# Weights requested by ScalarE, gradient rows requested two blocks ahead, and the inverse transform's last stage moved into the final tiles of the last chunk

## The chip, the cores and the metric

One core of one Trainium2 chip. The metric is the device time of one execution in microseconds. The engines are named as the profile names them: PE (TensorE, matmul), DVE (VectorE), ACT (ScalarE), POOL (GpSimd) and SP (SyncE, which here only requests transfers).

## The reference

The kernel computes a forward pass and its gradient. For x of 2048 tokens and D = 576 columns:

```python
xn = _layernorm(x)
out = x + S4(xn) + FFN(xn)
# S4: K = Re sum_n C exp(dt A l) dt B;  y = irfft(rfft(xn) * rfft(K)) + xn * Dskip
# FFN: h = relu(xn @ W_gate) * (xn @ W_up);  h @ W_down   (F = 4608)
out, vjp = jax.vjp(f, x, A_re, A_im, B_re, B_im, C_re, C_im, log_dt, Dskip, W_gate, W_up, W_down)
return out, *vjp(grad_out)
```

So there are 13 outputs: out (out_0), the gradient of x (out_1), those of the S4 parameters, and those of the three weight matrices.

## The kernel before

The work is written as two Python generators, and the main function takes from them in turns. `Ffn.gen` gives the feed-forward part, `S4.gen` the convolution; each `yield` hands over an estimate of the time of what was just written. After each piece of the FFN the main function takes pieces of S4 while S4's estimated time is behind `PACE` times the FFN's. The scheduler of the framework then orders each engine's instructions by itself, by the order of the program, the tiles' dependencies and the buffers of the pools; every transfer that an engine requests stands in that engine's order, and a request that has to wait holds up what stands behind it.

The FFN runs over 12 chunks of Fc = 384 hidden columns (three blocks ft of 128) and in each over 4 groups of 512 tokens. `load_w` (L211) requests a chunk's weights (five transfers), one chunk ahead, into one of two buffers. `a_unit` (matmuls at L254) makes the gate, the up projection and the gradient of h; `t_unit` (L278) transposes its results; `outdx` (matmuls at L296, 18 of 288 columns per tile of 128 tokens) adds a token tile's part of out and dx to `acc_dram` by a GpSimd transfer that accumulates. The weight gradients of a chunk follow at the start of the next one: `dw_down` four times (q = 0 to 3; 48 matmuls of 144 columns each, L316), `dw_gu` four times (L330, 32 matmuls of 384 columns) and `dw_left` (L346, which ends the chunk's work; its last one ends the kernel's matmuls). Each of these nine blocks requests its own rows, `gq_dram[q]` (L307) or `xs_dram[k]` (L326, L342), into a tile `rows` of the pool `ffn_d`, which has three buffers.

S4 is a convolution by discrete Fourier transforms of 16 x 256 points, done as matmuls in stages, with blocks that go out to DRAM and come back transposed between the stages (A, S, C). Everything is done for two halves of the columns, hf = 0 and 1, of DH = 288. `p1(hf)` transforms xn and the output gradient and ends with the gradient of the kernel K, `dk_dram`; `p2(hf)` makes K and the gradients by the parameters (`turn`, L880/L890; `sums`, L903 to L908, one turn per SC = 32 columns); `p3(hf)` multiplies in the frequency domain and transforms back. A last stage is a matmul pair of S3 and a block of C (`back2`, L658). `both` (L971) deals two of these out side by side by estimates of their lengths: p2(0) with p1(1) by W1, p2(1) with p3(0) by W3. p3(1) and `grads` come last. In p3's last stage (L733 to L751), for each half and each of 16 tiles, `base` = x + xn * Dskip + y (and the like for the gradient) is made on DVE from the pair in PSUM and stored to `base_dram` in FP32.

In the last chunk S4 is drained at the first outdx (the mark "last"), and from the third outdx on `final_tile(t)` is called, two tiles behind. It loads `f_base` (L1007), `f_acc` (L1009) and `f_xg` (L1011), adds, stores out (L1015), applies the layernorm's gradient, and stores dx (L1026). Tiles 10 to 15 are called between the last four dw_down and dw_gu.

`Balance.copy` decides by sums of estimates whether a copy out of PSUM goes to DVE (L62) or ACT (L68). PSUM has pools of 4 (`ps_mm`), 2 (`ps_s`, that of S4) and 2 (`pt`) banks.

Of the kernel before, what the change touches and what calls it, by code (L numbers as in the profile page):

```python
# [14 lines left out]
P = 128  # L15
# [7 lines left out]
ST = 16  # L23
# [11 lines left out]
PACE = 0.95  # L35
W1, W2, W3 = 56.0, 400.0, 91.0
# [145 lines left out]
class Ffn:  # L182
    def __init__(self, g, ctx, Wg, Wu, Wd, dWg, dWu, dWd):
# [20 lines left out]
        self.X = {}  # L204
        tail = D - (NK - 1) * P
# [5 lines left out]
    def load_w(self, c):  # L211
        nc = self.g.nc
        f0 = c * Fc
        nfull = NK - 1
        tail = D - nfull * P
        for w, W in ((self.wgs[c % 2], self.Wg), (self.wus[c % 2], self.Wu)):
            nc.sync.dma_start(w[:, 0:nfull, :], W[0:nfull * P, f0:f0 + Fc].rearrange("(k p) f -> p k f", p=P))
            nc.sync.dma_start(w[:tail, nfull, :], W[nfull * P:D, f0:f0 + Fc])
        nc.sync.dma_start(self.wds[c % 2][:, :, 0:D], self.Wd[f0:f0 + Fc, :].rearrange("(t p) d -> p t d", p=P))
# [102 lines left out]
    def dw_gu(self, c, k):  # L322
        g, nc = self.g, self.g.nc
        f0 = c * Fc
        xs = self.dp.tile([P, ST, 144], BF16, name="rows")
        nc.sync.dma_start(xs[:, :, 0:P], g.xs_dram[k][:])  # L326
# [8 lines left out]
    def dw_left(self, c):  # L335
# [5 lines left out]
        xs = self.dp.tile([P, ST, 144], BF16, name="rows")  # L341
        nc.sync.dma_start(xs[:, :, 0:W], g.xs_dram[k][:])  # L342
# [116 lines left out]
class S4:  # L459
    def __init__(self, g, aps, outs, Dskip):  # L460
# [8 lines left out]
        self.dk_dram = two("dk_dram", [P, ST, DH])  # L469
# [3 lines left out]
        self.base_dram = d("base_dram", [P, ST, 2, D], F32)  # L473
# [189 lines left out]
    def p1(self, hf):  # L663
# [28 lines left out]
        with ExitStack() as c:  # L692
            bp = self.pool(c, f"p1_c{hf}", 3)
            for n2 in range(ST):
                S3 = self.dft(bp, self.s3_dram, n2)
                Ct = bp.tile([P, 1, 2, DH], BF16, name="bC1")
                nc.sync.dma_start(Ct[:], self.C[1][hf][:, n2])
                o = bp.tile([P, DH], BF16, name="dk_o")
                g.bal.copy(o[:], self.back2(S3, Ct, 0), DH)
                nc.sync.dma_start(self.dk_dram[hf][:, n2, :], o[:])  # L700
                yield 0.3

    def p3(self, hf):
# [26 lines left out]
        with ExitStack() as c:  # L732
            cp = self.pool(c, f"p3_c{hf}", 1)  # L733
            dsk = cp.tile([P, DH], BF16, name="dsk")
            nc.sync.dma_start(dsk[:], self.Dskip[cols].rearrange("(o d) -> o d", o=1).to_broadcast([P, DH]))
            bp = self.pool(c, f"p3_d{hf}", 2)
            for n2 in range(ST):
                S3 = self.dft(bp, self.s3_dram, n2)
                Ct = bp.tile([P, 2, 2, DH], BF16, name="bC2")
                nc.sync.dma_start(Ct[:], self.C[2][hf][:, n2])  # L740
                xt = bp.tile([P, 3, DH], BF16, name="xt")
                nc.sync.dma_start(xt[:, 0, :], g.x_v[:, n2, cols])
                nc.sync.dma_start(xt[:, 1:3, :], g.xg_dram[:, n2, :, cols])
                o = bp.tile([P, 2, DH], F32, name="base")
                v.tensor_tensor(o[:], xt[:, 1:3, :], dsk[:].unsqueeze(1).to_broadcast([P, 2, DH]), op=ALU.mult)
                v.tensor_tensor(o[:, 0, :], o[:, 0, :], xt[:, 0, :], op=ALU.add)
                for i in range(2):
                    v.tensor_tensor(o[:, i, :], o[:, i, :], self.back2(S3, Ct, i), op=ALU.add)
                nc.sync.dma_start(self.base_dram[:, n2, :, cols], o[:])
                bal.add(d=1.8)  # L750
                yield 1.8  # L751
# [408 lines left out]
```

## Time and profile before

| what | value |
|---|---|
| median of 9 runs | 2060.55 us (2054.33 to 2063.26) |
| profiled execution | 2058.33 us |
| its span | 2056.6 us |
| mean granted clock | 0.972 |
| DMA, mean | 181 GB/s, 372.86 MB |

The profile is one execution, and its times count from the start of the span. A group's line gives the line, engine, operation and tile names, then the count, the busy time in us and the mean in ns, and behind the second bar the idle time of that engine just before these instructions and what ended most of it. In a line of windows, the numbers behind the times are busy us of PE, PE's weight loads, DVE, ACT and POOL. The chunks end, by dw_left, at about 199, 413, 595, 753, 908, 1069, 1226, 1388, 1542, 1726, 1897 and 2050 us, counted at the start of that work.

### The profile page before, as it was taken

What the parts mean: (1) busy time and instruction counts of PE and PEld (TensorE: products, weight loads), DVE (VectorE), ACT (ScalarE), POOL (GpSimd) and SP (SyncE); (2) the same over time, 40 slices, a digit from 0 to 9 for tenths busy, and PEclk for the clock granted to TensorE, in tenths of its full rate; (3) what the DMA queues carried; (4) which work ended last, traced back from release to release, by engine and by line L of the source; (5) the groups of instructions that cost most, each with busy time, mean ns of one, the idle gap of its engine ahead of it and who ended that gap; (6) DMA issues with size and microseconds to landing.
All of it is one profiled execution on the core that took longest, in us unless ns stands there. A gap on an engine that the chain in (4) does not pass through costs nothing.

```text
span 2056.6 us, 44413 instructions
## 1 busy us (share of the span) xinstructions
PE 1852.6 (90%) x16775; PEld 1261.5 (61%) x16919; DVE 1466.8 (71%) x3633; ACT 1468.3 (71%) x3244; POOL 256.8 (12%) x321
## 2 busy tenths in 40 slices
PE   5889897989999999998999999899999799788886
PEld 3665566556756766765766756666666565465563
DVE  6454862799988888896888778789887266554662
ACT  3665773799979879888879879868878545352552
POOL 4220110001101101101101101101101100110110
PEclk9999998989999999999999999999999999999997
DMA  9656888746755748747846755777755877986886
GB/s 321 208 183 179 248 221 224 196 135 129 184 142 127 189 137 180 160 126 183 184 140 126 176 149 117 185 191 188 184 123 111 215 207 217 260 193 191 216 237 170
DMA packets 390368, 372.86 MB, mean 181 GB/s; under 512 B 196042, under 2 KB 314058, under 8 KB 389898
## 3 DMA queue, kind: packets, MB, share of 16 engines
q1 hardware_dynamic: 358794, 303.95, 49.8%
q0 software_dynamic: 29248, 63.72, 20.0%
q8 instruction: 132, 2.16, 0.4%
q10 hardware_dynamic: 2112, 2.36, 0.3%
q14 instruction: 82, 0.67, 0.1%
HBM read 220.74 MB, written 149.20 MB: 180 GB/s over the span
## 4 chain that ended last, share of the span: by engine, by line
PE 40%; ACT 25%; DMA 15%; DVE 15%; issue 5%; SPq 1%; POOL 0%; ACTq 0%; DVEq 0%; POOLq 0%
PE ps_mm L330 10%; PE ps_mm L254 9%; PE ps_mm L296 7%; ACT osx L68 4%; ACT YT L68 2%; PE ps_s L625 2%; PE ps_mm L316 2%; DMA A_k<-fA 2%; DMA base_dram<-base 2%; PE ps_s L890 2%; ACT hN L68 2%; PE ps_s L626 2%; PE pt L278 1%; ACT ysn L831 1%; ACT ya L832 1%
## 5 line engine op out<-in xcount | busy, mean ns | idle before, releaser
L68 ACT CAST osx<-ps_mm 128x288 bf16<-128x288 f32 x716 | 280.1, 441 | 41.0 <-PE ps_mm L296 39.3
L301 POOL DMA_DIRECT2D acc_dram<-osx x176 | 153.2, 870 | 1193.5 <-ACT osx L68 819.4
L296 PE MATMUL ps_mm<-wgT,dgT 128*128 128x288 bf16 x1152 | 215.0, 287 | 5.7 <-DVE upm L261 3.1
L296 PE MATMUL ps_mm<-wuT,duT 128*128 128x288 bf16 x1152 | 215.3, 288 | 0.0
L330 PEld LDWEIGHTS <-rows 128*128 128x128 bf16 x1536 | 148.0, 98 | 98.7 <-DMA rows<-xs_dram 7.9
L254 PE MATMUL ps_mm<-xT,wg 128*128 128x512 bf16 x591 | 186.0, 394 | 11.4 <-ACT osx L68 3.8
L296 PE MATMUL ps_mm<-wd,hT 128*128 128x288 bf16 x1152 | 191.2, 287 | 4.4 <-ACT osx L68 1.6
L254 PE MATMUL ps_mm<-xT,wu 128*128 128x512 bf16 x714 | 193.1, 389 | 0.4
L254 PE MATMUL ps_mm<-gT,wdT 128*128 128x512 bf16 x711 | 185.2, 382 | 8.2 <-DVE upm L261 6.3
L316 PE MATMUL ps_mm<-rows,hN 128*128 128x144 bf16 x2304 | 166.1, 232 | 14.3 <-DMA rows<-gq_dram 13.3
L261 DVE SCALAR_TENSOR_TENSOR upm<-rg,ps_mm 128x512 bf16<-128x512 bf16 x144 | 98.6, 685 | 109.1 <-PE ps_mm L254 72.9
L316 PEld LDWEIGHTS <-hN 128*128 128x128 bf16 x2304 | 156.6, 101 | 19.1 <-DMA rows<-gq_dram 10.2
L68 ACT COPY YT<-ps_s 128x1024 bf16<-128x1024 bf16 x139 | 142.9, 1028 | 17.1 <-PE ps_s L890 16.0
L330 PE MATMUL ps_mm<-dgN,rows 128*128 128x384 bf16 x768 | 147.1, 330 | 7.7 <-DMA rows<-xs_dram 7.7
L68 ACT CAST dhb<-ps_mm 128x512 bf16<-128x512 f32 x144 | 86.3, 599 | 91.6 <-PE ps_mm L254 91.4
L330 PE MATMUL ps_mm<-duN,rows 128*128 128x384 bf16 x768 | 142.4, 327 | 0.1
L907 DVE TENSOR_TENSOR pr<-X,ps_s 128x256 f32<-128x256 f32 x288 | 109.3, 417 | 44.8 <-PE ps_s L903 44.2
L296 PEld LDWEIGHTS <-dgT 128*128 128x128 bf16 x1152 | 111.0, 98 | 37.8 <-issue 11.7
L296 PEld LDWEIGHTS <-duT 128*128 128x128 bf16 x1152 | 112.2, 98 | 30.7 <-issue 3.0
L296 PEld LDWEIGHTS <-hT 128*128 128x128 bf16 x1152 | 107.3, 98 | 35.6 <-issue 8.9
L254 PEld LDWEIGHTS <-wdT 128*128 128x128 bf16 x720 | 70.6, 99 | 88.2 <-issue 13.5
L254 PEld LDWEIGHTS <-wu 128*128 128x128 bf16 x720 | 70.5, 100 | 73.4 <-issue 10.4
(244 smaller groups left out, 4185.5 us busy)
## 6 DMA issues: line engine op xcount, KB each, us to landing
acc_dram<-osx POOLq DMA_DIRECT2D x192, 288.0 KB, 4.8
gT<-gT_dram SPq DMA_DIRECT2D x44, 640.0 KB, 6.4
xT<-xT_dram SPq DMA_DIRECT2D x44, 640.0 KB, 5.7
rows<-gq_dram SPq DMA_DIRECT2D x48, 576.0 KB, 4.7
rows<-xs_dram SPq DMA_DIRECT2D x48, 512.0 KB, 4.5
out_dram<-obw SPq DMA_DIRECT2D x96, 96.0 KB, 2.7
A_ug<-fA SPq DMA_DIRECT2D x32, 288.0 KB, 2.8
b_ug<-A_ug SPq DMA_DIRECT2D x32, 288.0 KB, 4.0
```

What stands on the lines that cost most here:

```text
L68: self.nc.scalar.copy(out, in_)
L254: nc.tensor.matmul(ps[:], lhsT=w[:, k, fs], rhs=rhs[:, k, :], start=(k == 0), stop=(k == NK - 1))
L261: nc.vector.scalar_tensor_tensor(upm[:], rg[:], 0.0, ps_u[:], op0=ALU.is_gt, op1=ALU.mult)
L278: nc.tensor.transpose(out=pt[:, j, :], in_=src[:, j * P:(j + 1) * P], identity=g.ident_bf[:])
L296: nc.tensor.matmul(ps[:, :DH], lhsT=lt[:, js], rhs=rh, start=(i == 0), stop=(i == len(mms) - 1))
L301: nc.gpsimd.dma_start(g.acc_dram[:, t, :, :], o[:], accum_op=ALU.add)
L316: nc.tensor.matmul(ps[:, (ft - f) * 144:(ft - f + 1) * 144], lhsT=self.hN[:, st, ft * P:(ft + 1) * P], rhs=gq[:, st, :], start=(st == 0), ...
L330: nc.tensor.matmul(ps[:, :Fc], lhsT=xs[:, st, 0:P], rhs=src[:, st, :], start=(st == 0), stop=(st == ST - 1))
L625: nc.tensor.matmul(ps[:, :DH], lhsT=CC[:], rhs=src[:, o, :], start=True, stop=False)
L626: nc.tensor.matmul(ps[:, :DH], lhsT=sm[:], rhs=src[:, other, :], start=False, stop=True)
L890: nc.tensor.transpose(out=tb[:, i * P:(i + 1) * P], in_=Y[:, ri, dl, :], identity=g.ident_bf[:])
L907: nc.vector.tensor_tensor(pr[:], X[:, dx:dx + DG, r0:r0 + 2].rearrange("p d r a -> p d (r a)").unsqueeze(2).to_broadcast(sh), psg[:, 0:DG ...
```

## The change

Five edits are made together.

1. `PACE` goes from 0.95 to 0.9, and `W3` from 91 to 62.
2. `load_w` requests on ACT (`nc.scalar`) and not on SP.
3. A new function `Ffn.rows(c, i)` gives the rows of a block; it requests those of blocks i, i + 1 and i + 2 if they have not been requested. The tile is written contiguously, also where a row block is narrower than the buffer.
4. p1's last stage writes its 16 blocks into one tile `dk` and stores that once; S3 comes from a pool of its own with 2 buffers, and `dk_dram` gets a layout in which `dkr` is loaded in whole lines.
5. p3's last stage and `base_dram` are gone. `S4.base(pools, t)` does this work for a whole tile of 576 columns, and `final(t)` calls it for tiles t to t + 2; x is added in PSUM by a matmul with the identity, the sum stays in SBUF as `f_base`, and `f_xg` is handed on to `final_tile`.

The diff, cut:

```diff
-PACE = 0.95
-W1, W2, W3 = 56.0, 400.0, 91.0
+PACE = 0.9
+W1, W2, W3 = 56.0, 400.0, 62.0
...
-            nc.sync.dma_start(w[:, 0:nfull, :], W[0:nfull * P, f0:f0 + Fc].rearrange("(k p) f -> p k f", p=P))
+            nc.scalar.dma_start(w[:, 0:nfull, :], W[0:nfull * P, f0:f0 + Fc].rearrange("(k p) f -> p k f", p=P))
...
+    def rows(self, c, i):
+        g, nc = self.g, self.g.nc
+        for n in range(i, min(i + 3, 4 + NK)):
+            if (c, n) not in self.R:
+                t = self.dp.tile([P, ST, 144], BF16, name="rows")
+                src = g.gq_dram[n] if n < 4 else g.xs_dram[n - 4]
+                w = 144 if n < 4 else min(P, D - (n - 4) * P)
+                v = t[:].rearrange("p t d -> p (t d)")[:, 0:ST * w].rearrange("p (t d) -> p t d", d=w)
+                nc.sync.dma_start(v, src[:])
+                self.R[(c, n)] = v
+        return self.R[(c, i)]
...
-        gq = self.dp.tile([P, ST, 144], BF16, name="rows")
-        nc.sync.dma_start(gq[:], g.gq_dram[q][:])
+        gq = self.rows(c, q)
...
+            dk = self.pool(c, f"p1_d{hf}", 1).tile([P, DH // SC, ST, SC], BF16, name="dk")
+            sp = self.pool(c, f"p1_e{hf}", 2)
             for n2 in range(ST):
-                S3 = self.dft(bp, self.s3_dram, n2)
+                S3 = self.dft(sp, self.s3_dram, n2)
...
-                o = bp.tile([P, DH], BF16, name="dk_o")
-                g.bal.copy(o[:], self.back2(S3, Ct, 0), DH)
-                nc.sync.dma_start(self.dk_dram[hf][:, n2, :], o[:])
+                g.bal.copy(dk[:, :, n2, :], self.back2(S3, Ct, 0).rearrange("p (g d) -> p g d", d=SC), DH)
                 yield 0.3
+            nc.sync.dma_start(self.dk_dram[hf][:], dk[:])
...
+    def base(self, pools, t):
...
+        S3 = two.tile([P, 2, P], BF16, name="S3")
+        nc.sync.dma_start(S3[:], self.s3_dram[:, t])
+        Ct = two.tile([P, 2, 2, 2, DH], BF16, name="bC2")
+        for hf in range(2):
+            nc.sync.dma_start(Ct[:, hf], self.C[2][hf][:, t])
+        xt = two.tile([P, D], BF16, name="xt")
+        nc.sync.dma_start(xt[:], g.x_v[:, t, :])
+        xg = three.tile([P, 2, D], BF16, name="f_xg")
+        nc.sync.dma_start(xg[:], g.xg_dram[:, t])
+        o = three.tile([P, 2, D], F32, name="f_base")
+        v.tensor_tensor(o[:], xg[:], self.dsk[:].unsqueeze(1).to_broadcast([P, 2, D]), op=ALU.mult)
+        for i in range(2):
+            for hf in range(2):
+                cols = slice(hf * DH, (hf + 1) * DH)
+                ps = self.ps()[:, :DH]
+                for ri in range(2):
+                    nc.tensor.matmul(ps, lhsT=S3[:, ri, :], rhs=Ct[:, hf, i, ri, :], start=(ri == 0), stop=(ri == 1 and i == 1))
+                if i == 0:
+                    nc.tensor.matmul(ps, lhsT=g.ident_bf[:], rhs=xt[:, cols], start=False, stop=True)
+                v.tensor_tensor(o[:, i, cols], o[:, i, cols], ps, op=ALU.add)
...
+        for n in range(t, min(t + 3, ST)):
+            if n not in bases:
+                bases[n] = s4.base(fin, n)
```

The new pools are `fin1` (the Dskip row), `fin2` (S3, bC2, xt: two buffers each) and `fin3` (f_xg, f_base, f_acc, f_o, f_m: three each).

How it moves instructions, at three places. First SP near the end of the kernel, before the change. out_0 and out_1 are the stores of final tiles, f_base, f_acc and f_xg their loads, out_12 the stores of dW_down; the number behind a name tells buffers apart (f_o_32145 is tile 11's, f_acc_32232 tile 13's).

```order
L1026 DMA out_1_dram<-f_o_32145 128x576
L1015 DMA out_0_dram<-f_o_32164 128x576
L1009 DMA f_acc_32232<-acc_dram_98 128x1152
L1011 DMA f_xg_32234<-xg_dram_86 128x1152
L307 DMA rows_32249<-gq_dram3_97 128x2304
L1015 DMA out_0_dram<-f_o_32236 128x576
L1026 DMA out_1_dram<-f_o_32164 128x576
L1007 DMA f_base_32302<-base_dram_156 128x1152
L320 DMA out_12_dram<-obd_32016 128x3x288
```

And after (f_o_31871 is tile 11's, f_acc_32078 tile 14's; S3, bC2 and xt are loads of the new stage):

```order
L1030 DMA f_acc_32078<-acc_dram_98 128x1152
L1045 DMA out_1_dram<-f_o_31871 128x576
L313 DMA rows_31787<-gq_dram3_97 128x2304
L759 DMA xt_31889<-in_A_u_dram 128x576
L761 DMA f_xg_31891<-xg_dram_86 128x1152
L754 DMA S3_31884<-s3_dram_139 128x256
L757 DMA bC2_31886<-C_ydu0_148 128x1152
L757 DMA bC2_31886<-C_ydu1_149 128x1152
L1034 DMA out_0_dram<-f_o_31915 128x576
L333 DMA out_12_dram<-obd_31692 128x3x288
L313 DMA rows_31928<-xs_dram0_89 128x2048
```

The rows of q = 3 stood four places behind tile 11's store of out_1 and stand right behind it now. The first rows of xs come eight places later, with loads of the new stage between; before they came thirteen places later, outside the rows shown. f_acc is requested one tile further ahead.

Second, DVE in the middle of the last chunk's final tiles, before (L1014 to L1025 are a final tile's):

```order
L1022 TENSOR_SCALAR f_m_31762<-f_m_31762,rinv_81 128x1
L1023 SCALAR_TENSOR_TENSOR f_base_31752<-f_xg_31756,f_m_31762,f_base_31752 128x576
L1017 TENSOR_TENSOR f_base_31799<-f_base_31799,f_acc_31801 128x576
L1020 SCALAR_TENSOR_TENSOR f_acc_31801,f_m_31809<-f_base_31799,f_xg_31803 128x576
L1025 TENSOR_TENSOR f_o_31758<-f_base_31752,f_xg_31756 128x576
L1021 TENSOR_SCALAR f_m_31809<-f_m_31809 128x1
L1022 TENSOR_SCALAR f_m_31809<-f_m_31809,rinv_81 128x1
L1023 SCALAR_TENSOR_TENSOR f_base_31799<-f_xg_31803,f_m_31809,f_base_31799 128x576
```

And after (L772 adds a result of the new stage, L1033 to L1044 are a final tile's):

```order
L772 TENSOR_TENSOR f_base_30482<-f_base_30482,ps_s4_30498 128x288
L772 TENSOR_TENSOR f_base_30511<-f_base_30511,ps_s4_30513 128x288
L1040 TENSOR_SCALAR f_m_30537<-f_m_30537 128x1
L1041 TENSOR_SCALAR f_m_30537<-f_m_30537,rinv_81 128x1
L1042 SCALAR_TENSOR_TENSOR f_base_30453<-f_xg_30451,f_m_30537,f_base_30453 128x576
L772 TENSOR_TENSOR f_base_30511<-f_base_30511,ps_s4_30518 128x288
L772 TENSOR_TENSOR f_base_30511<-f_base_30511,ps_s4_30523 128x288
L1033 TENSOR_TENSOR f_o_30605<-f_base_30482,f_acc_30603 128x576
L772 TENSOR_TENSOR f_base_30511<-f_base_30511,ps_s4_30527 128x288
L1044 TENSOR_TENSOR f_o_30533<-f_base_30453,f_xg_30451 128x576
```

The new stage's additions stand among the final tiles' operations, one and two tiles ahead of them, so an operation that waits here holds up both.

Third, weight requests, on SP before (xT, gT are the FFN's inputs; s_ug, b_k and C_ydu blocks of S4):

```order
L217 DMA wg0_102<-in_B_W_gate_dram 128x4x384
L218 DMA wg0_102<-in_B_W_gate_dram 64x384
L217 DMA wu0_104<-in_B_W_up_dram 128x4x384
L241 DMA xT_20482<-xT_dram_87 128x2560
L730 DMA C_ydu0_148<-fC2_18897 128x1152
L243 DMA gT_20484<-gT_dram_88 128x2560
L218 DMA wu0_104<-in_B_W_up_dram 64x384
L720 DMA b_k_20080<-A_k0_140 128x576
L219 DMA wd0_106<-in_B_W_down_dram 128x3x576
```

And on ACT after, for an earlier chunk's weights:

```order
L68 CAST osx_10501<-ps_mm_10507 128x288
L855 ACTIVATE ya_11057<-yr_11058 128x512
L218 DMA wg1_103<-in_B_W_gate_dram 128x4x384
L68 CAST osx_10501<-ps_mm_10520 128x288
L68 CAST osx_10544<-ps_mm_10545 128x288
L68 CAST osx_10544<-ps_mm_10550 128x288
L68 CAST osx_10544<-ps_mm_10555 128x288
```

The requests left SP, where they stood among other requests, and now stand on ACT among copies out of PSUM (osx, L68) and the S4 activations.

More of the change, by code (lines that the diff above doesn't have):

```diff
@@ L204, in __init__ @@
         self.X = {}
+        self.R = {}
         tail = D - (NK - 1) * P
@@ L731, in p3 @@
                 yield 1.5
[L732 to L751, printed above, removed]
@@ L998, in gen, with final_tile @@
         yield from self.grads()
-def final_tile(g, s4, pool, small, t):
+def final_tile(g, base, xg, pool, small, t):
     nc, bal = g.nc, g.bal
     inv_d = 1.0 / D
-    base = pool.tile([P, 2, D], F32, name="f_base")
-    nc.sync.dma_start(base[:], s4.base_dram[:, t])
     acc = pool.tile([P, 2, D], BF16, name="f_acc")
     nc.sync.dma_start(acc[:], g.acc_dram[:, t])
-    xg = pool.tile([P, 2, D], BF16, name="f_xg")
-    nc.sync.dma_start(xg[:], g.xg_dram[:, t])
     xn, gt = xg[:, 0, :], xg[:, 1, :]
```

29 lines of the change are left out of this document (18 added, 11 removed).

## The prediction

> **What bounds the kernel now.** I read the page first, then the windows, then the waits in the windows where TensorE is idle.
>
> ```profile
> PE 1852.6 (90%) x16775; PEld 1261.5 (61%) x16919; DVE 1466.8 (71%) x3633; ACT 1468.3 (71%) x3244; POOL 256.8 (12%) x321
> ```
>
> TensorE is busy for 90% of the span of 2056.6 us, so an edit can gain only where the other 204 us lie. The busy time in eight stretches (columns: start:end, length, then busy time and instructions of each engine, granted clock, DMA share, GB/s):
>
> ```profile
> 320.00:356.00 36.00, 22.74 (x245) 19.22 (x243) 4.03 (x9) 10.28 (x24) 1.70 (x2) 0.85 0.80 206
> 413.00:595.00 182.00, 166.97 (x1657) 115.44 (x1670) 166.40 (x398) 163.55 (x349) 22.51 (x22) 0.96 0.58 142
> 1310.00:1470.00 160.00, 146.62 (x1443) 103.33 (x1453) 132.45 (x298) 119.65 (x248) 17.95 (x19) 0.98 0.77 197
> 1470.00:1595.00 125.00, 120.03 (x1283) 84.65 (x1291) 96.73 (x228) 101.09 (x210) 16.08 (x17) 1.00 0.60 134
> 1735.00:1805.00 70.00, 55.13 (x394) 35.76 (x398) 39.71 (x88) 32.50 (x72) 6.90 (x8) 0.95 0.93 251
> 1805.00:1897.00 92.00, 79.41 (x649) 54.98 (x652) 46.89 (x175) 39.84 (x97) 8.00 (x10) 0.96 0.73 177
> 1899.70:1995.00 95.30, 79.12 (x562) 50.94 (x568) 64.57 (x143) 61.70 (x142) 12.92 (x15) 0.95 0.88 237
> 1995.00:2052.40 57.40, 40.98 (x355) 29.39 (x352) 16.78 (x34) 12.27 (x25) 0.91 (x2) 0.82 0.66 178
> ```
>
> Three limits show. In 413:595 VectorE (166.40) and ScalarE (163.55) are as full as TensorE: the S4 transforms there set the pace. In 320:356, 1735:1805 and 1995:2052.4 nobody is full and the DMA share is high: transfers are waited for. In 1470:1595 TensorE is nearly alone, idle for 5.0 of 125, or 4.0%. The change works on all of them, and moves work from the second kind into the last chunk (1899.7 to the end, 152.7 us up to 2052.4).
>
> **The change part by part.** The sum is made against the profiled execution, 2058.33 us (span 2056.6 and 1.7 around it). The median of nine is 2060.55, so 2.2 is added at the end.
>
> T1, the last stage of p3 leaves the steady part. Its two halves lie in 1310:1470 and 1735:1805. A matmul of 288 columns is priced from this piece of the chain, and what the stage waits for on VectorE from its groups (busy us, mean ns; idle before):
>
> ```profile
> 1086.19 2.21 PE ps_mm L296 x18
> L748 DVE TENSOR_TENSOR base<-base,ps_s 128x288 f32<-128x288 f32 x64 | 26.6, 449 | 5.5 <-PE ps_s L658 5.4
> L745 DVE TENSOR_TENSOR base<-xt,dsk 128x576 f32<-128x576 bf16 x32 | 24.2, 757 | 43.5 <-DMA xt<-xg_dram 31.9 <-DMA base_dram<-base 11.5
> L746 DVE TENSOR_TENSOR base<-base,xt 128x288 f32<-128x288 f32 x32 | 14.6, 455 | 0.5
> ```
>
> 2.21/18 is 0.123 us; 128 of them go, 15.7 us of TensorE. That much is certain, the lower end. On top comes TensorE's idle time above what the neighbouring stretch has: 13.4 of 160 in 1310:1470 against 4.0% (6.4) is 7.0 more; 14.9 of 70 in 1735:1805 is 5.3 more than at the 13.7% of 1805:1897 (12.6 of 92), and 12.1 more than at 4.0%. The waits of L745 for its transfers, 43.5 us in all, say that this idle time belongs to the stage. 15.7 + 7.0 + 5.3 = 28. With 12.1 in place of 5.3, and 8.9 more if 1805:1897 falls to 4.0% idle too, it is 44. I take 30, nearer to the first, since 1805:1897 has its idle share without the stage. **−30** (−16 to −44).
>
> T2, p1's last stage writes its 16 small blocks into one tile and stores it once, with S3 in a pool of its own. Its wait is seen in the chain around 338 us:
>
> ```profile
> 338.19 3.13 DMA bC<-C_dk
> 344.98 2.75 DMA bC<-C_dk
> 350.14 4.76 DMA rows<-gq_dram
> ```
>
> In 320:356 TensorE idles 36.00 − 22.74 = 13.3 us; these three pieces are 10.6 of it. The bC loads stay, with fewer stores on SP between them; the rows load is now requested two blocks earlier. **−8** (0 to −13). The other half of p1 runs beside p2 and gets nothing.
>
> T3, the pace. S4 work is now started only while it is behind 0.90 of the FFN's estimated time, not 0.95, and W3, the length of p3 by which it is dealt out beside p2(1), falls from 91 to 62, which is 16 × 1.8 less, the stage that left. Between the second and third dw_left the order has 19 parameter-gradient turns where it had 23. A turn's VectorE work is two each of the first two groups, one each of the rest:
>
> ```profile
> L907 DVE TENSOR_TENSOR pr<-X,ps_s 128x256 f32<-128x256 f32 x288 | 109.3, 417 | 44.8 <-PE ps_s L903 44.2
> L908 DVE TENSOR_REDUCE Sm<-pr 128x8 f32<-128x256 f32 x288 | 108.3, 413 | 0.0
> L826 DVE TENSOR_TENSOR ya<-Tt,qv 128x512 f32<-128x512 f32 x144 | 99.9, 694 | 3.2 <-ACT ycs L833 2.9
> L828 DVE SCALAR_TENSOR_TENSOR yr<-yr,ya 128x512 f32<-128x512 f32 x144 | 99.2, 689 | 1.7
> L823 DVE TENSOR_TENSOR yE<-ex 128x512 bf16<-128x512 f32 x144 | 99.0, 689 | 2.1 <-ACT ex L792 0.4
> ```
>
> 0.834 + 0.826 + 0.694 + 0.689 + 0.689 = 3.73 us, four turns 15 us, out of a stretch where VectorE was 91% busy. The work is only put off, to stretches such as 1470:1595 where VectorE is 77% busy and has 28 us free, so a part may come back, not more than all. **−8** (0 to −15).
>
> T4, the weight loads change engine. Five requests a chunk go from SP to ScalarE; ten chunks ask while others run. The time of one issue on each engine (ns min/median/max), what SP waited for in front of them, and the page's group of the matmuls that use the gate weights:
>
> ```profile
> L124 ACTq DMA_DIRECT2D g<-in_grad_out_dram x4: 374/374/457, 0.8 to 42.4; - x4
> L218 SPq DMA_DIRECT2D wg<-in_B_W_gate_dram x12: 471/516/1552, 1.7 to 1632.7; - x12
> SPq L217 <- PE ps_mm L254: 30.3, 8, 13.9
> SPq L219 <- PE ps_mm L296: 22.1, 7, 11.5
> L254 PE MATMUL ps_mm<-xT,wg 128*128 128x512 bf16 x591 | 186.0, 394 | 11.4 <-ACT osx L68 3.8
> ```
>
> 50 × 0.374 to 0.516 is 19 to 26 us of ScalarE, under cover wherever it has room and exposed where it is 90% busy (413:595). The waits of 30.3 and 22.1 us for the buffers to come free now stand in ScalarE's own order, ahead of copies out of PSUM that TensorE waits for; only where the scheduler has put the request late enough do they vanish. What goes is SP's same time, for the requests behind it. That can gain little: of L254's 11.4 us of idle time 3.8 are ScalarE's, which leaves 7.6 that a load could have ended. **+8** (−8 to +30; nearer to the low end, as the requests stand in ScalarE's order behind copies that come after the same matmuls). Of the first ten, 10 × 0.374 = 3.7 us stand at the start, in the same range. The Trainium skill (DMA: Bandwidth & Descriptors, "Issuing engines are not separate DMA queues") says that requests of all engines run on the same 16 DMA engines, and that another issuer saves no more than the time to initiate. By that the move itself gains nothing; the sum here already gives it no gain.
>
> T5, rows requested up to two blocks ahead. Between chunks they had cover before, apart from the load of T2. At the tail they had not; that lies in T6. The sizes and times of these loads, and of two that go (KB each, median us to landing):
>
> ```profile
> rows<-gq_dram SPq DMA_DIRECT2D x48, 576.0 KB, 4.7
> rows<-xs_dram SPq DMA_DIRECT2D x48, 512.0 KB, 4.5
> base_dram<-base SPq DMA_DIRECT2D x32, 288.0 KB, 4.0
> f_base<-base_dram SPq DMA_DIRECT2D x16, 576.0 KB, 6.1
> ```
>
> The second lands in 128x16 pieces of 256 B, the first in whole lines of 4,608 B; per KB it takes 8% more (8.8 ns against 8.2); so landing xs in whole lines is put at **0** (0 to −1 at the tail). The Trainium skill (the same page, "Why small descriptors are slow") puts 27% of overhead on a piece of 256 B; by it the load would be an estimated 1.0 us shorter (4.5 − 4.5/1.27), of which the two rows show a third.
>
> T6, the last chunk, which takes the stage in. Each of 16 tiles gets 10 matmuls of 0.123 us (19.6 us in all, in a chunk where TensorE has 152.7 − 79.12 − 40.98 = 32.6 us idle), six loads where it had three, and on VectorE one multiplication of 1152 elements and four additions of 288. By L746 and L745 an element costs (757 − 455)/288 = 1.05 ns, so the multiplication is 0.757 + 576 × 1.05 ns = 1.36 us, the additions 4 × 0.449 = 1.80, together 3.16. The rows of block q3 are requested behind tile 11's last store, as before; by then bases 0 to 13 have been made, three of their multiplications before the chunk. VectorE's work up to there is 64.57 + 14 × 3.16 − 3 × 1.36 = 104.7 us. What follows it is read from these rows of the end:
>
> ```profile
> 2002.52 0.76 DVE L1014 TENSOR_TENSOR f_o<-f_base,f_acc 128x576 bf16<-128x576 f32 x1 [8.06 <-DMA f_acc<-acc_dram]
> 2003.20 0.75 DVE L1025 TENSOR_TENSOR f_o<-f_base,f_xg 128x576 bf16<-128x576 f32 x1
> 2013.00 5.48 PE L316 MATMUL ps_mm<-rows,hN 128*128 128x144 bf16 x48 [8.73 <-DMA rows<-gq_dram]
> 2026.17 5.30 PE L330 MATMUL ps_mm<-dgN,rows 128*128 128x384 bf16 x16 [7.69 <-DMA rows<-xs_dram]
> 2026.17 23.58 PE ps_mm L330 x128
> 2049.76 2.74 PE ps_mm L346 x32
> ```
>
> From the end of tile 11's L1025 (2003.95) to the matmuls on q3 are 9.1 us; from 2013.00 to 2052.4 another 39.4, of which the wait of 7.69 goes, since xs is asked for ahead; two more bases on TensorE are 2.5. Together 43.3. The chunk then takes 104.7/u + 43.3, u being VectorE's busy share. In this chunk now u is 64.57/95.30 = 0.68, but set by waits for transfers and TensorE, not by VectorE's load; in 1310:1470 it is 132.45/160 = 0.83, with the same stage beside the FFN; in 413:595 it is 0.91. At 0.83 the chunk takes 126.1 + 43.3 = 169.4, **+17**; at 0.91, 158.4, +6; at 0.68, 197.3, +45. I take 0.83, because the bases are asked for two tiles ahead, which gives VectorE work that does not wait for f_acc, as in L1014's 8.06.
>
> Sum: −30 − 8 − 8 + 8 + 0 + 17 = −21, so 2037 profiled, **2039 us** as a median.
>
> **The rivals.**
>
> A, slower: the last chunk becomes VectorE's. Every tile's outdx result, its additions and its final tile run in one order on VectorE, and the row request and everything after it stand behind tile 11. If u stays at today's 0.68, T6 is +45, the sum +7: 2067. It decides over the others from T6 = +38, u = 104.7/(190.7 − 43.3) = 0.71. For it: today's row 1899.7:1995 has u = 0.68 with a DMA share of 0.88, and the base stage itself had to wait 43.5 us for its loads. Against it: the load of f_base, the largest of a tile (576 KB), goes from this chunk.
>
> B, no change: weight requests hold ScalarE up, T4 = +30. The sum is +1: 2061. For it: ScalarE at 163.55 of 182 and the 52 us of waits. Against it: a request that is placed late does not wait. Under this head falls also that the lead on the rows changes nothing, because their buffers come free late.
>
> C, a larger gain: transfers had slowed their neighbours too. T1 −44, T2 −13, T3 −8, T4 0, T6 +6: −59, 2001. For it: a DMA share of 0.93 in 1735:1805 with TensorE idle, and the stores and loads of base gone (32 × 288 KB and 16 × 576 KB, 18.4 MB). Against it: 1805:1897 idles 13.7% of the time without the stage.
>
> **How the numbers follow.** A difference of 0.2%, about 4 us, is what a measurement of this kernel can tell from no change. My forecast (2015 to 2056) has a chance of 0.53. C (below 2015) has 0.17; by sign both are faster, 0.70. B, within 4 us of 2060, has 0.11. A, above 2065, has 0.19. The range reaches from 2008, midway from the forecast's edge to C's 2001, to 2068, just above A's price; about 0.09 is left out below and 0.10 above. The forecast's own range is 2015 to 2056.
>
> **What would show it.** T1: no work named base before the last chunk, and TensorE idle for about 4% where 1310:1470 had 8.4%. T2: TensorE's idle time around 320 to 356 down by half. T3: the chunk from 413 to 595 shorter by some 8 us. T4: ScalarE's row of weight requests without waits of several us in front of copies out of PSUM. T6: a last chunk of 160 to 180 us, VectorE above 0.8 until tile 11, and no wait of 7.69 for rows of xs. The last chunk should begin 38 us earlier than now, at 1862. The forecast is wrong if it takes over 190 us, or begins later than 1875.

## The result and the profile after

The changed kernel takes 2014.77 us (median of 10 runs, 2010.04 to 2019.47) where the kernel before takes 2060.05 (31 runs). The ratio is 0.9784, 95% interval [0.977, 0.9799]: 44.5 us less, where 21 were forecast. The time lies inside the wide range (2008 to 2068) and 0.2 us below the forecast's own (2015 to 2056). In what follows the runs are given as ratios to the kernel before on the same chip, and as us by that ratio of 2060.

By dw_left the last chunk began at 1832.8 and not at 1897.0, so the earlier chunks gained 64 us where 38 were forecast. The last one grew from 152.7 to 168.7, by 16 where 17 were forecast. These are two single executions; that of the changed kernel (2010.0) is the fastest of the ten, so the two figures add up to 48 and not to 44.5. The page, and windows of the changed kernel (columns as above):

```profile
PE 1834.3 (91%) x16810; PEld 1257.1 (63%) x16951; DVE 1457.6 (73%) x3602; ACT 1459.6 (73%) x3227; POOL 256.1 (13%) x321
DMA packets 214125, 348.19 MB, mean 173 GB/s; under 512 B 34266, under 2 KB 131930, under 8 KB 213402
```

```profile
320.00:356.00 36.00, 28.11 (x304) 23.06 (x304) 3.21 (x7) 12.88 (x33) 5.07 (x5) 0.95 0.82 231
411.50:579.80 168.30, 156.49 (x1551) 108.45 (x1560) 145.90 (x338) 146.76 (x316) 19.24 (x20) 0.99 0.58 147
1668.30:1832.80 164.50, 149.12 (x1153) 97.63 (x1166) 97.36 (x328) 89.16 (x223) 14.90 (x18) 0.98 0.70 180
1835.50:1958.10 122.60, 101.92 (x733) 67.36 (x740) 94.17 (x199) 66.37 (x147) 13.83 (x16) 0.92 0.82 219
1958.10:2004.20 46.10, 39.00 (x342) 28.09 (x339) 24.93 (x52) 11.78 (x24) 0.00 (x0) 0.93 0.67 204
```

The traffic fell from 372.86 to 348.19 MB. 411.5:579.8 is the stretch that was 413:595; it lost 13.6 us, and VectorE is 87% busy in it, not 91%. 1668.3:1832.8 answers to 1726.1:1897.0 of before. The last two rows are T6's two parts, up to tile 11's last operation and from there, 122.6 + 46.1 = 168.7; forecast were 126.1 + 43.3. The costs per operation came out as worked out: a multiplication 1.356 us (1.36), an addition 0.451 (0.449):

```profile
L772 DVE TENSOR_TENSOR f_base<-f_base,ps_s 128x288 f32<-128x288 f32 x64 | 26.7, 451 | 8.7 <-PE ps_s L771 4.5 <-PE ps_s L769 4.0
L763 DVE TENSOR_TENSOR f_base<-f_xg,dsk 128x1152 f32<-128x1152 bf16 x16 | 21.6, 1356 | 27.9 <-DMA f_xg<-xg_dram 27.8
```

So the length of the last chunk came out nearly as forecast, and the excess lies in what the edits gave to the earlier chunks. Which edit gave it?

### The profile page after: what moved, and what is told of

Same layout as the page of the kernel before. It is cut to its first block, busy times and chain, and to the rows that moved or that the text cites. A ratio compares the mean times of both kernels' runs of the same rounds, so it can differ in the third digit from the quotient of the medians.

```text
span 2008.3 us, 44064 instructions
## 1 busy us (share of the span) xinstructions
PE 1834.3 (91%) x16810; PEld 1257.1 (63%) x16951; DVE 1457.6 (73%) x3602; ACT 1459.6 (73%) x3227; POOL 256.1 (13%) x321
## 2 busy tenths in 40 slices
DMA packets 214125, 348.19 MB, mean 173 GB/s; under 512 B 34266, under 2 KB 131930, under 8 KB 213402
## 3 DMA queue, kind: packets, MB, share of 16 engines
q0 software_dynamic: 29248, 63.72, 20.7%
## 4 chain that ended last, share of the span: by engine, by line
PE 42%; ACT 24%; DVE 16%; DMA 12%; issue 5%; SPq 0%; POOL 0%; ACTq 0%; DVEq 0%; POOLq 0%
PE ps_mm L255 11%; PE ps_mm L342 9%; PE ps_mm L297 7%; ACT osx L68 4%; ACT YT L68 2%; PE ps_s L635 2%; PE ps_mm L329 2%; ACT hN L68 2%; PE ps_s L913 2%; ACT dgN L68 2%; PE ps_s L636 2%; PE ps_mm L357 1%; DMA bC<-C_dk 1%; ACT duN L68 1%; ACT ysn L854 1%
## 5 line engine op out<-in xcount | busy, mean ns | idle before, releaser
L68 ACT CAST osx<-ps_mm 128x288 bf16<-128x288 f32 x725 | 280.2, 441 | 37.1 <-PE ps_mm L297 34.4
L255 PE MATMUL ps_mm<-xT,wg 128*128 128x512 bf16 x592 | 179.3, 387 | 6.8 <-issue 1.5
L329 PE MATMUL ps_mm<-rows,hN 128*128 128x144 bf16 x2304 | 161.8, 229 | 4.6 <-DMA rows<-gq_dram 4.6
L68 ACT COPY YT<-ps_s 128x1024 bf16<-128x1024 bf16 x137 | 141.3, 1032 | 23.3 <-PE ps_s L913 22.7
L297 PEld LDWEIGHTS <-duT 128*128 128x128 bf16 x1152 | 112.0, 98 | 27.8 <-issue 0.5
L68 ACT CAST dhb<-ps_mm 128x512 bf16<-128x512 f32 x144 | 85.6, 594 | 58.9 <-PE ps_mm L255 56.6
```

The costliest lines, as they stand in the source:

```text
L68: self.nc.scalar.copy(out, in_)
L255: nc.tensor.matmul(ps[:], lhsT=w[:, k, fs], rhs=rhs[:, k, :], start=(k == 0), stop=(k == NK - 1))
L297: nc.tensor.matmul(ps[:, :DH], lhsT=lt[:, js], rhs=rh, start=(i == 0), stop=(i == len(mms) - 1))
L329: nc.tensor.matmul(ps[:, (ft - f) * 144:(ft - f + 1) * 144], lhsT=self.hN[:, st, ft * P:(ft + 1) * P], rhs=gq[:, st, :], start=(st == 0), ...
```

## The experiments

**Four edits undone, one at a time.** "Undone" means that the lines of the diff for that edit, and no others, are as before.

undo_base puts p3's last stage back, and W3 with it:

```diff
-W1, W2, W3 = 56.0, 400.0, 62.0
+W1, W2, W3 = 56.0, 400.0, 91.0
...
-                bases[n] = s4.base(fin, n)
...
+                for i in range(2):
+                    v.tensor_tensor(o[:, i, :], o[:, i, :], self.back2(S3, Ct, i), op=ALU.add)
+                nc.sync.dma_start(self.base_dram[:, n2, :, cols], o[:])
```

> The changed kernel with p3's last stage put back into p3, base_dram and W3 = 91 with it; all other edits kept. The changed kernel stands at -45 us against before, of which the last chunk's growth is +16 in the profile and the earlier chunks' gain -64. If the theory holds that T1 was as forecast (-30 + 16), this kernel stands at -45 + 14 = -31. If the rival holds that the whole excess of the earlier chunks (26 us over the forecast's 38) was T1, because the stage's loads and stores slowed everything beside them, it stands at about -5.

undo_pace:

```diff
-PACE = 0.9
+PACE = 0.95
```

> The changed kernel with PACE = 0.95 again (W3 stays 62). T3 as forecast (-8): the kernel stands at -37 against before, and the chunk between the second and the third dw_left is 8 us longer than in the changed kernel. Rival, the pace carries the excess (-25 or so, in several chunks): -20.

undo_weights:

```diff
-            nc.scalar.dma_start(w[:tail, nfull, :], W[nfull * P:D, f0:f0 + Fc])
+            nc.sync.dma_start(w[:tail, nfull, :], W[nfull * P:D, f0:f0 + Fc])
```

> The changed kernel with the weights requested by SP again. T4 as forecast (+8): it stands at -53 against before. Rival, requests by ScalarE gained, because SP no longer waits for the weight buffers (30.3 and 22.1 us in before) ahead of other requests: it stands at -35 or less. Third: no difference, -45.

undo_rows:

```diff
-        gq = self.rows(c, q)
+        gq = self.dp.tile([P, ST, 144], BF16, name="rows")
+        nc.sync.dma_start(gq[:], g.gq_dram[q][:])
```

> The changed kernel with each row block requested by its own block again, in the old layout of the tile. Theory: the lead gives only the waits it takes away, 16 us at the tail (8.73 and 7.69 in before) and some 5 around 350 us; against before the kernel stands at about -30 to -38. Rival, the lead gains 2 us or more in every chunk: -20 or less.

Measured: undo_base 0.9978 [0.9962, 0.9993], −4.5 us; undo_pace 0.9856 [0.9838, 0.9874], −30; undo_weights 0.9787 [0.977, 0.9804], −44; undo_rows 0.985 [0.9834, 0.9867], −31. So undoing the stage costs 40 us, the pace 15, the rows 14, the weights nothing that can be told from noise. The four together are more than the whole, so some depend on each other. undo_base shows on what:

```profile
1673.10:1889.10 216.00, 179.39 (x1304) 114.57 (x1303) 117.10 (x347) 104.94 (x264) 13.83 (x16) 0.91 0.77 213
```

Its chunk before the last takes 216 us where the changed kernel's takes 164.5: with the stage in p3, the slower pace leaves p3(1)'s transform, its last stage and the parameter gradients all to that chunk.

**Two edits undone together, and edits alone.** undo_base_pace has both of the first two edits undone. only_base (with W3 = 62) and only_rows are the kernel before with that one edit made. undo_p1 has p1's last stage as before:

```diff
-            nc.sync.dma_start(self.dk_dram[hf][:], dk[:])
+                nc.sync.dma_start(self.dk_dram[hf][:, n2, :], o[:])
```

> The changed kernel with p3's last stage back in p3 and PACE = 0.95; left of the change are ScalarE's weight requests, the rows' lead and p1's single store. Known: both edits undone one at a time cost 40 (stage) and 15 us (pace). Theory N, the two belong together: with the stage in p3 the slower pace leaves S4 work over, which is drained late (the chunk before the last grew to 216 us), so the stage alone is worth 14 as forecast, and this kernel stands at -30 + 14 = about -15 against before. Rival: both gains are their own and add up: +10.

> The kernel before with the stage moved into the final tiles (and W3 = 62), nothing else. Theory N: the forecast's T1 + T6, -30 + 16 = -14 (somewhat less, since the last chunk has no rows' lead). Rival, the stage itself is worth what its undoing costs: -40.

> The kernel before with the rows requested two blocks ahead in a contiguous tile, nothing else. Theory: the tail's two waits (8.73 and 7.69 us) and the 4.76 us at 350 us go, -10 to -20 against before; the undoing cost 14. Rival, the gain comes only with the changed kernel's last chunk or its order: 0 to -5.

> The changed kernel with p1's last stage as before (16 stores of dk_o, one pool) and dk_dram in the old layout. T2 as forecast (-8): it stands at -37 against before. Rival: no difference, -45, since the bC loads (10.4 us of TensorE's waits in the changed kernel, 9.4 before) and not the stores were waited for.

Measured: undo_base_pace 0.9955 [0.9938, 0.9972], −9; only_base 0.9863 [0.9844, 0.9881], −28; only_rows 0.9934 [0.9911, 0.9956], −14; undo_p1 0.9786 [0.9767, 0.9805], −44. Now there is a path without a gap: rows, weights and p1 give 9; the stage on top 20 (alone 28); the pace on top 15, 44.5 in all. p1's single store gives nothing. With the stage in p3 the slower pace loses about 5, which is hardly clear of noise (undo_base against undo_base_pace, whose intervals just overlap); with the stage out it gains 15. Theory N is right that the two belong together. It is not right on the stage, which is worth 20 to 28 by itself, not 14, though the last chunk of only_base takes 169.5 us, a growth of 17. So T1, the stage in its old place, was too small.

Two more edits depend on each other. The slower pace without the rows' lead (undo_rows, −31) is hardly better than the stage alone (only_base, −28), and so is the lead without the slower pace (undo_pace, −30); only both together give 44.5. (undo_rows and undo_pace also have the weights and p1, which cost nothing when undone.) So the 15 of the pace and the 14 of the rows are for the most part the same gain. And the lead shortens the last chunk only while the stage is elsewhere: in the profiles it takes 141.6 us in only_rows where before took 152.7, but with the stage in it 169.5 without the lead (only_base) and 169.4 with it (undo_pace).

**Why did the stage cost more? A chain of waits?** Two kernels leave it in p3 and ease its waits, before_spread and before_deep:

```diff
-                yield 1.8
+                yield (1.8, 4.4)[hf]
```

```diff
-            bp = self.pool(c, f"p3_d{hf}", 2)
+            bp = self.pool(c, f"p3_d{hf}", 2 + 2 * hf)
```

> The kernel before; only the estimate of a tile in p3's last stage is 4.4 and not 1.8 in the second half, so that more FFN work is dealt out between two of its 16 tiles. Theory L: the second half of the stage, which stood alone beside the FFN (70 us in 1735 to 1805, 4.4 us a tile by its transfers, with 30 us of FFN work dealt to it), cost by a chain of latencies per tile for which the FFN was not given enough work; with 4.4 us dealt the tiles' waits are covered and the kernel gains 10 to 20 us against before, the stage staying where it is. Rival: the stage's cost is its work and its DMA load (share 0.93), wherever it stands: no gain, 0 to -3.

> The kernel before with four buffers and not two for the tiles of p3's last stage in its second half. Theory L in the form that the buffers set the chain (a load waits until two tiles before it are stored): -10 or more. Rival, the chain is SP's order, in which a store that waits for VectorE stands ahead of the next tile's loads: 0 to -3.

Measured: 1.0012 [0.9995, 1.003] and 0.9992 [0.9974, 1.001]. Neither gains, so theory L is not borne out in either form. With more FFN work dealt to it, the second half of the stage only took longer, from the chunk's end to its own 86.2 us where before took 79 (1726 to 1805), at a DMA share of 0.92:

```profile
1718.80:1805.00 86.20, 73.74 (x526) 45.64 (x533) 48.70 (x112) 42.91 (x97) 8.63 (x10) 0.98 0.92 256
```

**Its parts taken away.** Four kernels leave out parts of the stage, and with them y or more in out and dx; in all four the final tiles load a block of the same size as before.

stage_dma_only keeps the loads, and stores a constant tile; `v.tensor_tensor` and `back2` go:

```diff
-                    v.tensor_tensor(o[:, i, :], o[:, i, :], self.back2(S3, Ct, i), op=ALU.add)
-                nc.sync.dma_start(self.base_dram[:, n2, :, cols], o[:])
+                nc.sync.dma_start(self.base_dram[:, n2, :, cols], oo[:])
```

stage_compute_only does the work, on the first tile's loads:

```diff
+                if n2 == 0:
+                    Ct = cp.tile([P, 2, 2, DH], BF16, name="bC2")
+                    nc.sync.dma_start(Ct[:], self.C[2][hf][:, n2])
...
+                if n2 == ST - 1:
+                    nc.sync.dma_start(self.base_dram[:, n2, :, cols], o[:])
```

stage_gone_yields keeps of the loop only this, and stage_gone not the yield (nor W3 = 91) either:

```diff
+                if n2 == ST - 1:
+                    nc.sync.dma_start(self.base_dram[:, n2, :, cols], oo[:])
+                bal.add(d=1.8)
+                yield 1.8
```

> The kernel before; p3's last stage keeps all its loads and its stores (of a constant tile), and its matmuls and VectorE's operations are left out, so y and the Dskip term are missing from out and dx. Moving the stage alone gained 28 us, of which the last chunk's growth had taken 17 in the profile, so the stage in its old place cost some 45. Theory D, its transfers cost (DMA share 0.93 beside it): little is gained, 0 to -12. Theory C, a chain on in-order engines (load, VectorE, TensorE, VectorE, store): -30 to -45. Theory W, its work on TensorE and VectorE in their order: -30 to -45 too.

> The kernel before; p3's last stage does all its matmuls and VectorE's operations on the first tile's loads and stores only the last tile, so out and dx are made from wrong blocks. Theory D: -30 to -45. Theory C: -25 or more. Theory W: 0 to -10.

> The kernel before without p3's last stage: no loads, no matmuls, no VectorE work, one store of a constant tile per half; the final tiles read that block, so y, x and the Dskip term are missing from out and dx. The estimates of 1.8 a tile are still dealt, so the FFN gets the same share beside it. Known: transfers alone gone -20, work alone gone -13 (in the first half either gives 12, in the second only the transfers 11). Theory A, the stage's price is all in its transfers and work: -45. Theory B, part of the price is that S4's sequence is longer by 57.6 of estimates and ends 130 us later: -25 to -33 here, the rest only when the estimates go too.

> As the kernel without the stage, but the 32 estimates of 1.8 are not dealt either, and W3 = 62, as in the kernel in which only the stage was moved. Theory A: no more than with the estimates, -45 in both. Theory B: -45 here, and 12 to 20 less gain with the estimates.

Measured: stage_dma_only 0.9936 [0.9914, 0.9958], −13; stage_compute_only 0.9901 [0.9882, 0.992], −20; stage_gone_yields 0.9775 [0.9748, 0.9802], −46; stage_gone 0.9811 [0.9784, 0.9837], −39. So the stage cost 39 to 46 us in its old place (only_base's 28 and the 17 by which its last chunk grew give 45), and not because S4's list is longer by it: theory A. Theories D, C and W each expected one of the two parts to carry most of it; none of them fits, since leaving out the work gives 13 and the transfers 20. Where it cost shows in windows over two chunks each (single executions; that of before is some 10 us longer than the medians beside these runs, so the costs add up to a little over 46), the pair with the first half of the stage and the pair with the second. Before, then transfers alone, work alone, and nothing left:

```profile
1226.20:1541.80 315.60, 295.83 (x2921) 206.37 (x2944) 265.41 (x618) 252.02 (x530) 40.79 (x42) 0.99 0.69 167
1541.80:1897.00 355.20, 310.58 (x2496) 204.92 (x2519) 196.18 (x573) 189.21 (x454) 28.68 (x34) 0.97 0.77 197
```

```profile
1224.10:1527.60 303.50, 289.58 (x2882) 201.75 (x2882) 238.64 (x555) 250.40 (x530) 40.77 (x42) 0.98 0.69 173
1527.60:1882.00 354.40, 308.51 (x2456) 201.21 (x2455) 165.91 (x510) 188.92 (x454) 28.68 (x34) 0.93 0.75 198
```

```profile
1224.00:1529.00 305.00, 293.87 (x2947) 204.03 (x2946) 265.65 (x618) 251.59 (x530) 41.46 (x42) 1.00 0.56 130
1529.00:1872.60 343.60, 312.45 (x2520) 204.34 (x2519) 192.37 (x573) 187.05 (x454) 28.68 (x34) 0.97 0.67 167
```

```profile
1226.90:1521.90 295.00, 285.55 (x2883) 198.22 (x2882) 239.91 (x555) 250.76 (x530) 40.44 (x42) 1.00 0.57 132
1521.90:1846.90 325.00, 301.11 (x2458) 197.28 (x2459) 165.31 (x510) 186.81 (x454) 28.75 (x34) 0.98 0.69 174
```

First half: 315.6 with all, 303.5 with the transfers, 305.0 with the work, 295.0 with neither; the two costs, 8.5 and 10.0, add up to 18.5 of 20.6. Second half: 355.2, 354.4, 343.6, 325.0; the transfers alone cost 29.4, as much as the whole stage (30.2), though TensorE uses nothing of them, and the work alone costs 18.6. The two overlap there. How transfers alone cost so much, stage_dma_only's own trace shows, in windows of 20 us, a wait of TensorE (total in us, times, longest) and its place on the timeline:

```profile
1730.00:1750.00 20.00, 19.62 (x144) 12.30 (x143) 4.86 (x10) 12.67 (x29) 3.45 (x4) 1.00 1.08 294
1750.00:1770.00 20.00, 9.87 (x83) 6.58 (x81) 2.64 (x6) 8.84 (x20) 1.72 (x2) 0.80 1.07 319
1770.00:1790.00 20.00, 8.73 (x30) 4.05 (x30) 4.71 (x18) 4.19 (x9) 0.00 (x0) 0.59 0.71 220
```

```profile
PE ps_mm L254 <- DMA xT<-xT_dram: 15.4, 1, 15.4
```

```profile
1776.52 2.29 PE L254 MATMUL ps_mm<-xT,wg 128*128 128x512 bf16 x5 [15.39 <-DMA xT<-xT_dram]
```

The stage's transfers fill the DMA engines (1.08, 1.07) and SP's order; the FFN's next xT is requested at 1771.5, right behind the stage's last store (1770.9), and TensorE waits 15.4 us for it. The granted clock in the 20 us that follow is 0.59.

In the kernel before it is another wait. There TensorE waits only 1.8 us for xT and gT in the chunk before the last, and 12.1 us at the stage's own matmuls, for VectorE and for the loads of C:

```profile
PE ps_s L658 <- DVE base L748: 6.9, 5, 2.3
PE ps_s L658 <- DMA bC<-C_ydu: 5.2, 2, 3.0
```

So that the stage cost 39 to 46 us is shown; how much of it goes to which wait in the kernel before is not.

**The last chunk.** after_few_adds and after_loads_once leave out work of the moved stage (the first leaves out most of y; the second uses tile 0's S3, bC2 and x for every tile, and still loads f_xg); after_loads_act requests its loads on ScalarE:

```diff
-                v.tensor_tensor(o[:, i, cols], o[:, i, cols], ps, op=ALU.add)
+                c8 = slice(hf * DH, hf * DH + 8)
+                v.tensor_tensor(o[:, i, c8], o[:, i, c8], ps[:, 0:8], op=ALU.add)
```

```diff
+        if t == 0:
+            S3 = one.tile([P, 2, P], BF16, name="S3")
+            nc.sync.dma_start(S3[:], self.s3_dram[:, t])
...
+            self.once = S3, Ct, xt
+        S3, Ct, xt = self.once
```

```diff
-        nc.sync.dma_start(xg[:], g.xg_dram[:, t])
+        nc.scalar.dma_start(xg[:], g.xg_dram[:, t])
```

> The changed kernel, but the four additions per tile of the moved stage are made on 8 columns of 288 only, so most of y is left out of out and dx. Theory V, the last chunk is VectorE's: 56 additions before tile 11's end are some 0.3 us shorter, 17 us of work, at VectorE's share of 0.77 there -22 us against the changed kernel (about -66 against before). Rival, the last chunk waits for f_acc (SP waits 37.8 us for the accumulated sums) and for TensorE: -5 or less (about -50).

> The changed kernel; S3, bC2 and xt are loaded for tile 0 only and used for all tiles, so y and x are wrong in out and dx. It asks what made the last chunk 16 us longer, since the additions of VectorE did not. Theory D, the moved stage's loads (88 requests on SP, 13.7 MB): the last chunk loses 8 us or more of its growth, -53 or more against before. Theory W, TensorE's 19.6 us of matmuls: -45 to -48.

> The changed kernel with the six loads of the moved stage (S3, two of bC2, xt, f_xg, once Dskip) requested by ScalarE and not SP. Theory V: no gain, since VectorE's work stays, and some 90 issues of 0.4 us lie on ScalarE, 36 us, where it is 54% busy: 0 to +5 against the changed kernel (-40 to -45 against before). Rival, the loads stand on SP behind its waits for f_acc (37.8 us): -5 to -10 more (-50 to -55).

Measured: 0.9807 [0.978, 0.9834], 0.9805 [0.9781, 0.983] and 0.9864 [0.9839, 0.989]: no gain from fewer additions, none from fewer loads, and 16 us lost with the loads on ScalarE, 10 of them in the last chunk (178.8 us in the profile). The last chunk of the first two, behind the changed kernel's:

```profile
1832.80:2001.50 168.70, 140.91 (x1074) 95.44 (x1081) 120.08 (x253) 78.26 (x170) 13.83 (x16) 0.92 0.79 218
```

```profile
1831.40:1998.40 167.00, 140.87 (x1072) 96.44 (x1079) 103.65 (x253) 77.79 (x170) 13.82 (x16) 0.92 0.79 221
```

```profile
1832.00:1999.20 167.20, 140.86 (x1082) 96.67 (x1083) 119.69 (x253) 78.17 (x170) 13.86 (x16) 0.92 0.59 153
```

VectorE has 16 us less to do in the first, the DMA share is 0.59 in the second, and the chunk loses 1.7 and 1.5 us. Neither was its limit. The rows above show what grew: TensorE's busy time, from 79.12 + 40.98 to 101.92 + 39.00, by 20.8 us, while its idle time fell from 32.6 to 27.8. The 160 matmuls of the stage were forecast at 19.6. No run leaves them out, so this is read from the rows and not tested. And nearly all of the idle time stands in front of the stage's own matmuls:

```profile
PE ps_s L769 <- DVE f_base L772: 17.5, 8, 5.9
PE ps_s L769 <- DMA bC<-C_ydu: 6.4, 3, 3.8
```

VectorE in turn waits for f_xg (27.8 us in front of L763, in the row above). It still does so when the additions are short, when the other loads are gone and when ScalarE requests it (16.5, 20.6 and 19.6 us in the last chunk, 15.7 in the changed kernel). f_xg has three buffers and is now read up to the end of its final tile; on SP its request follows that tile's store (1958.8 and 1959.3). That more buffers for it would shorten the chunk is a guess that no run here tries.

**The pace further down.**

```diff
-PACE = 0.9
+PACE = 0.85
```

> The changed kernel with PACE = 0.85. With the stage out, the pace from 0.95 to 0.9 gained 15 us, with the stage in it lost 5. Theory: S4 must be done before the drain at the end of the chunk before the last; in the changed kernel its last work is at 1753 of 1833, and a pace of 0.85 puts it off by about 100 us, past that: slower than the changed kernel by 5 to 20, -25 to -40 against before. Rival, a slower pace always relieves the full engines: -50.

Measured: 0.9845 [0.9822, 0.9867], −32, as the theory had it, 13 worse than at 0.9. The last chunk takes 198 us, and parameter gradients run in it on VectorE (the second row is a group of the window from 1817 to 1900):

```profile
1816.90:2015.10 198.20, 152.47 (x1081) 99.60 (x1080) 142.44 (x354) 89.74 (x202) 14.91 (x18) 0.85 0.74 208
```

```profile
L964 DVE TENSOR_TENSOR q<-Gd,raw 128x128 f32<-128x128 f32 (+1 forms) x14 | 3.9, 287 | 8.1 <-ACT g_ob L956 7.3 <-DMA raw<-in_A_B_re_dram 0.8
```

Of the kernels that leave no work out none is faster than the changed one; undo_weights and undo_p1 equal it.

## Why the prediction was right in direction and half the size

The direction was right, and so was the length of the last chunk, by luck (T6); the gain was 44.5 and not 21. With the measured terms the prediction's own sum comes out: −46 + 0 − 15 + 0 + 0 + 16 = −45.

- **T1 is the step that failed**: "15.7 + 7.0 + 5.3 = 28". The stage cost 46 in its old place, where 30 were taken: 16 of the 23.5 us that the forecast was short. In the windows above, idle time of TensorE falls by 10.3 and 20.7 us, where 7.0 and 5.3 were put down to the stage, and busy time by 10.3 and 9.5 where it was 7.85 each. The 5.3 came from taking off 13.7%, the idle share of 1805:1897, as if that stretch were undisturbed: in before TensorE idles 15.1 + 12.6 us in the two parts of the chunk before the last (1726.1:1805 and 1805:1897), in stage_gone_yields 8.8 in the whole of it. And the idle time was looked for in two short windows. The upper end, 44, was the better value. Rival C had it, and 2014.8 falls just under its edge of 2015; its T4 (0) was right too, but its T2 (−13) and T6 (+6) were further off than the forecast's.
- **T2** (−8) was nothing. The bC loads were waited for, and still are; 320:356 went from 13.3 to 7.9 us of idle time, but undoing the single store costs nothing. What was gained up to the third dw_left came with the rows and the pace together: undo_rows reaches its third dw_left 11 us later than the changed kernel (590.8 and 579.8), and its last chunk is only 2 us longer. That T2's miss of 8 and T4's cancel in the sum was luck.
- **T3** (−8) was −15, but not by the relieved stretch alone. That gained 12 us (180.1 in undo_pace, 168.3 in the changed kernel), the chunks up to 1668.3 gained 22 more, and the chunk before the last gave 24.5 back (140.0 and 164.5): the work was put off, as the prediction said, but mostly to there. The gain holds only with the stage gone (otherwise about +5, hardly clear of noise) and with the rows ahead. That these edits depend on each other was not seen.
- **T4** (+8) was nothing. ScalarE's requests took 0.37 to 0.49 us in the median, and of the 24 at L218 only 2 had a wait for a semaphore put in front of them; on SP (L217 before, the same line of the program) it was 10 of 24:

```profile
L218 ACTq DMA_DIRECT2D wg<-in_B_W_gate_dram x12: 369/370/529, 1.3 to 1579.4; - x12
L218 ACTq EVENT_SEMAPHORE  x2: 17/17/17, 1579.0 to 1581.9; - x2
L217 SPq EVENT_SEMAPHORE  x10: 17/17/17, 124.1 to 1624.1; - x10
```

  undo_weights has SP wait 93.8 us in front of its weight requests (49.0, 35.1 and 9.7), where it was 30.3 and 22.1 in before, and takes the same time as the changed kernel; so SP's waits there held up nothing that mattered. On ScalarE the longest pause of the copies around the two semaphores is 2.1 us (1580.5 to 1582.6). That ScalarE comes to the other requests late enough is argued from the missing semaphores. The Trainium skill (DMA: Bandwidth & Descriptors, "Issuing engines are not separate DMA queues") says that another issuer saves only the time to initiate. 0.9787 against 0.9784 agrees with it.
- **T5**: nothing for the whole lines, as taken. The xs rows land in 4.7 us, 4.5 before:

```profile
rows<-xs_dram SPq DMA_DIRECT2D x48, 512.0 KB, 4.7
```

  The estimate of 1.0 us less from the Trainium skill (the same page, "Why small descriptors are slow") isn't borne out. The lead itself is worth 14 alone, of which the last chunk has 11 (152.7 to 141.6 in only_rows). T6 counted 7.7 of that, the wait for xs, but with the stage in the last chunk that wait is gone without the lead too (undo_rows has none there). Outside the last chunk the lead was put at nothing; with the slower pace it gave 11 us up to the third dw_left.
- **T6** (+17) was +16, but not for the reason given. VectorE's share was 0.77 and its work up to tile 11 was 94 us, not 105 (fewer of the stage's operations had been done by then: 48 additions and 10 multiplications, where 56 and 11 were counted); the two errors met, which is luck. As after_few_adds shows, the chunk's length isn't VectorE's work over a share: by the rows it grew with TensorE's work, of whose 19.6 us T6 put only 2.5 into the sum. The share of before, 0.68, was also misread: its window ends at 1995, 9 us before tile 11's last operation. Up to 2004 VectorE is busy for 66.05 of 104.3 us, 0.63, and with that A's price would have been near +58 and not +45. Rival A, by which the last chunk would be VectorE's, is out; rival B is out with T4.

Along the path: rows, weights and p1 9 us, the stage 20, the pace 15. The stage gains less on this path than alone because the rows' lead had already shortened the last chunk (139.0 us in undo_base_pace), and moving the stage in takes that back.

## What to carry to other kernels

A stage that runs beside a matmul stream can cost more than its own matmuls and the idle time in its window: here 46 us, where 28 were read from the trace. Its transfers alone cost 33 of these and its work alone 26, so the two overlap; size such a stage by taking it out, not by its idle time less a neighbour's. A neighbour just behind a congested stage is no undisturbed reference. A pace between two streams has to be set again after a stage moves: 0.9 gained 15 us with the stage out and lost some 5 with it in, and 0.85 lost 13 again, with parameter gradients left over for the last chunk. And a forecast that comes out right in one term should be checked for its reason: T6 was right by two errors.

## What was not expected of the hardware

Sixty transfers moved from one engine's queue to another's changed nothing measurable (0.9787 against 0.9784), but the five loads per tile moved onto ScalarE in the last chunk cost 16 us; why is not shown. 512 KB landed as fast in pieces of 256 B (4.5 us) as in pieces of 4 KB (4.7 us), though the page counts 196,042 packets under 512 B before and 34,266 after (the layout of dk_dram has a part in that too).
